# Retention followed by a Fourier-mixing layer on one Trainium2 core: the first batch of the kernel is rebuilt

## The chip, the cores and the metric

The kernel runs on one core of one Trainium2 chip. The metric is the device time of one execution in microseconds (us). The time is the median of several runs; beside it there is one execution taken by the hardware profiler, from which the profile and the trace come.

The engines are named as in the profile: PE is TensorE (matrix products and transposes by an identity), DVE is VectorE, ACT is ScalarE, POOL is GpSimd and SP is SyncE, which here only issues transfers. PSUM is the memory that PE writes to; the other engines read it from there.

## The reference

There are two parts. The first is a recurrent attention over q, k, v of 4 batches x 8 heads x 768 steps x 64 features. The second is a mixing layer on its output x, 768 x 512 per batch. Cut to what is computed:

```python
# for each batch and head; gamma[h] = 1 - 2**(-5-h)
for t in range(768):
    state = gamma * state + outer(k[t], v[t])         # 64 x 64
    y[t] = (q[t] @ state) / 8
x = heads of y side by side                            # 768 x 512
u = x + real(fft(fft(x, axis=seq), axis=feature))
un = (u - mean(u)) / sqrt(var(u) + 1e-6)               # over the 512 features
out = u + relu(un @ w_ch1) @ w_ch2                     # 512 -> 2048 -> 512
```

All inputs and the output are f32. The kernel computes its matrix products in f16 with f32 sums.

## The kernel before

**Attention.** The sequence is cut into 6 chunks of 128 steps, and the 8 heads are taken as 4 pairs in the order 0, 1, 3, 2. For one pair of the first batch: q and k and v are loaded (L171, 384 KB each, on SP's queue), cast to f16 (q at L403, k in two halves with its decay at L412 or L419, v at L428 and L432), q and k are transposed on PE (L444) and copied from PSUM (L452, L455 on ACT). The products k q of each chunk (L469) are masked by the decay on DVE (L476, tile atm). The products k v of the chunks (L491) run through a scan on DVE (L500), which gives the state before each chunk (s16). The output of a head is the sum of atm x v (L515) and q x state (L531) in one PSUM tile, and ACT brings it to the x tile (L544). In the x tile the features 0 to 256 lie forward (side 0) and the others backward (side 1), so that a real transform can be folded.

**The transform.** DVE adds and subtracts the halves of the sequence (fold_s, L684) and the two sides (fold_d, L694). Stage 1 (s1, L741) multiplies the folded x by the tables of cosines and sines over the sequence (csp, ssp), in four groups: cosine and sine, each for two halves of 128 features, and each group in six matmuls 193 wide. The result goes to the f16 tile g (L748 on ACT, L750 on DVE), and reversed to gr (L757). A small product of the edge column (g0_b, L784) gives the features' zero term. Stage 2 (s2, L854 and L858) multiplies a block of 128 rows of g by the tables over the features (cd16, sd16); blocks 0 to 2 of the six row blocks use g and 3 to 5 use gr. In the first batch x is added by PE for blocks 0 to 2 (px, L808, by half identities), and by POOL for the others (L875, L877). ACT copies the odd part (qn, L862, L866), DVE makes u (L867, L869).

**The layer.** The rows of u are centred (mean from an ACT sum, L722 and L728; un, L891), transposed (L945), copied to unT (L947, L948, L950, L952), multiplied by w1 (h0, L978 in the first half of the first batch, L961 later), passed through relu (L985 on ACT, L987 on DVE; L965, L967 later) to ht, and multiplied by w2 (ch, L1000). DVE scales by the deviation and adds u (L1004). In the first half of the first batch the h0 units take one row block at a time: three blocks with four groups of 16 matmuls each, 128 wide. w1 and w2 come in four parts each by transfers that POOL issues (L1154, L1161).

**Tables.** Before, DVE computes the reduced angles in fifteen operations (trig_dve, L294, L296, L298), three for each of five table parts, and ACT takes the absolute value and the sine and cosine (t_act, L322, L326, L331). csp and ssp are stored with even and odd columns apart, so that s1 reads 193 adjacent elements. A second cosine table in natural order, csn (L307), serves g0_b.

**The order.** Everything of the first batch up to its first layer products is listed in first_units(). After each unit pin() ties every instruction to the one before it on its engine, so each engine runs this list in the order that is written. Behind it emit(streams) sorts the units of all batches by due times that are written in the code; the h0 units stand there in the stream "majors" of batch 0. Between units the list holds fillers (L157): matmuls of a zeroed tile (wz, set by POOL at L208) into an unused PSUM tile, forty of them, 512 wide. Batches 1 and 2 take the same transform, batch 3 another form of the layer products; both keep their code, except for what csp and ssp look like. The loads of the first batch are issued in the order q, k, v of each pair. Those of batch 1 (load_unit with `after`) wait for a weight transfer and for an h0 matmul.

These are the lines that set the two table reads:

```python
nc.tensor.matmul(ps[:, par, :], eo[...], tab[:, par, sb, :], ...)   # L741, s1, 193 wide
nc.tensor.matmul(ps[:, kb, :], csn[:, sb, P * kb:P * kb + P], xg[:, sb, :], ...)   # L784
```

Of the kernel before, what the change touches and what calls it, by code (L numbers as in the profile page):

```python
# [18 lines left out]
P = 128  # L19
# [19 lines left out]
NPE = 2  # L39
MIX3 = ((0.005, 0.085, 0.110, 0.125, 0.150), (0.190, 0.290, 0.310, 0.325, 0.350),  # L40
# [9 lines left out]
def kernel(  # L50
# [13 lines left out]
    def pool(name, bufs, **kw):  # L64
# [25 lines left out]
    csp = const.tile([P, 2, 3, NK], f16, tag="csp")  # L90
    ssp = const.tile([P, 2, 3, NK], f16, tag="ssp")
    csn = const.tile([P, 3, 384], f16, tag="csn")
# [9 lines left out]
        "p (n w) -> p n w", n=4)  # L102
    pmask = const.tile([P, 4], f32, tag="pmask")
# [47 lines left out]
    wz = ht16[:, 0:2, :].rearrange("p a b -> p (a b)")[:, 0:DM]  # L151
    wps = ps_w.tile([P, DM], f32, tag="w", name="wps")

    def filler(n):
        def run():
            for _ in range(n):
                nc.tensor.matmul(wps, wz[:, 0:P], wz, start=True, stop=True)  # L157
        return run
# [5 lines left out]
    def load_unit(b, i, after=None):  # L164
        def run():
            h0 = 2 * PAIR_ORDER[i]
            for name, src in srcs.items():
# [18 lines left out]
    for i in range(4):  # L186
        load_unit(0, i)()
# [10 lines left out]
    kf_i = tmp[:, 0, 0:KN].bitcast(i32)  # L198
    kf = tmp[:, 1, 0:KN]
    rs = [tmp[:, 2 + n] if n < 4 else tmp2[:, n - 4] for n in range(10)]  # L200
    icoln = const.tile([P, 5], f32, tag="icoln")
    hpi = const.tile([P, 1], f32, tag="hpi")

    nc.gpsimd.iota(icol_i[:, 0:3], pattern=[[P, 3]], base=0, channel_multiplier=1)
    nc.gpsimd.iota(icol_i[:, 3:5], pattern=[[P, 2]], base=1, channel_multiplier=1)
    nc.gpsimd.iota(icol_i[:, 5:6], pattern=[[0, 1]], base=127, channel_multiplier=-1)
    nc.gpsimd.iota(kf_i, pattern=[[1, KN]], base=0, channel_multiplier=0)
# [5 lines left out]
    nc.vector.tensor_copy(icol[:, 0:6], icol_i[:, 0:6])  # L213
    nc.vector.tensor_scalar(out=gexp[:, 0], in0=lgrow, scalar1=icol[:, 3:4],
                            scalar2=float(math.log(0.125)), op0=ALU.mult, op1=ALU.add)
    nc.vector.tensor_scalar(out=gexp[:, 1], in0=lgrow, scalar1=icol[:, 5:6], scalar2=None,
                            op0=ALU.mult)
    nc.scalar.activation(gexp, gexp, AF.Exp, bias=0.0, scale=1.0)
    for h2 in range(2):
# [3 lines left out]
    make_identity(nc, ident16)  # L223
    nc.gpsimd.affine_select(out=maskf, in_=maskf, compare_op=ALU.is_ge, fill=0.0, base=0,
                            pattern=[[1, P]], channel_multiplier=-1)
    nc.gpsimd.memset(hpi, float(np.pi / 2))
    nc.gpsimd.memset(epsT, 1e-6)
    nc.gpsimd.memset(gk5[:, :, :, 0:1], 0.0)
    nc.vector.tensor_scalar(out=icoln[:, 0:3], in0=icol[:, 0:3],
                            scalar1=float(np.float32(1.0 / S)), scalar2=None, op0=ALU.mult)  # L230
    nc.vector.tensor_scalar(out=icoln[:, 3:5], in0=icol[:, 3:5], scalar1=float(1.0 / DM),
                            scalar2=None, op0=ALU.mult)
    nc.vector.tensor_copy(kf, kf_i)

    def gk_unit(hp):
        def run():
            nc.scalar.copy(gk5[:, hp, :, 1:], gk2[:, hp:hp + 1].unsqueeze(1).to_broadcast(
                [P, D, NCH - 2]))
        return run
# [49 lines left out]
    def trig_dve(idx, n, w, col, coln):  # L289
        r = rs[2 * idx][:, 0:w]  # L290
        ra = rs[2 * idx + 1][:, 0:w]

        def run():
            nc.vector.tensor_scalar(out=ra, in0=kf[:, 0:w], scalar1=coln, scalar2=MAGIC,  # L294
                                    op0=ALU.mult, op1=ALU.add)
            nc.vector.tensor_scalar(out=ra, in0=ra, scalar1=-MAGIC, scalar2=float(n),  # L296
                                    op0=ALU.add, op1=ALU.mult)
            nc.vector.scalar_tensor_tensor(out=r, in0=kf[:, 0:w], scalar=col, in1=ra,  # L298
                                           op0=ALU.mult, op1=ALU.subtract)
        return run  # L300

    def ts_dve(c):
        return trig_dve(c, S, KN, icol[:, c:c + 1], icoln[:, c:c + 1])

    def csn_unit(c):
        def run():
            nc.scalar.activation(csn[:, c, :], rs[2 * c + 1][:, 0:384], AF.Sin, bias=hpi,  # L307
                                 scale=-float(2.0 * np.pi / S))
        return run

    def td_dve(c):
        return trig_dve(3 + c, DM, 257, icol[:, 3 + c:4 + c], icoln[:, 3 + c:4 + c])

    def t_act(idx, part):
        w = KN if idx < 3 else 257
        r = rs[2 * idx][:, 0:w]
        ra = rs[2 * idx + 1][:, 0:w]
        sc = float(2.0 * np.pi / (S if idx < 3 else DM))

        def run():  # L320
            if part == 0:
                nc.scalar.activation(ra, r, AF.Abs, bias=0.0, scale=1.0)  # L322
            elif idx < 3:
                src = (ra, r)[part - 1].rearrange("p (i t) -> p t i", t=2)
                dst = (csp, ssp)[part - 1]
                nc.scalar.activation(dst[:, :, idx, :], src, AF.Sin,  # L326
                                     bias=hpi if part == 1 else 0.0,
                                     scale=-sc if part == 1 else sc)
# [20 lines left out]
    def x_edges(j):  # L349
        def run():  # L350
            nc.gpsimd.memset(xts[j][:, :, :, 0:2], 0.0)
            nc.gpsimd.memset(xts[j][:, :, :, 256:XW], 0.0)
        return run

    def half_ids():
        nc.gpsimd.tensor_scalar(out=hid, in0=ident16, scalar1=0.5, scalar2=1.0, op0=ALU.mult,
                                op1=ALU.mult)
        nc.gpsimd.tensor_scalar(out=nhid, in0=ident16, scalar1=-0.5, scalar2=1.0, op0=ALU.mult,
                                op1=ALU.mult)
# [4 lines left out]
    at, q16_of, kd_of, v16_of, last_cast = {}, {}, {}, {}, {}  # L364

# [33 lines left out]
    def q0_unit(i):  # L399
        def run():  # L400
            q16 = q16_of[0, i] = qzs[i % 2].rearrange("p h c d -> p (h c d)")[
                :, 0:NCH * P].rearrange("p (c h d) -> p c h d", c=NCH, h=2)
            nc.gpsimd.tensor_scalar(out=q16, in0=in_of.pop(("q", 0, i)).rearrange(  # L403
                "p h c d -> p c h d"), scalar1=1.0, scalar2=1.0, op0=ALU.mult, op1=ALU.mult)
        return run

    def k0_unit(i):
        def run():
            h0 = 2 * PAIR_ORDER[i]
            k32 = in_of.pop(("k", 0, i))  # L410
            kd = kd_of[0, i] = kp.tile([P, NCH, 2, D], f16, tag="kd16", name="kd16")
            nc.gpsimd.tensor_scalar(out=kd[:, :, 0, :], in0=k32[:, 0], scalar1=gkd[:, h0:h0 + 1],  # L412
                                    scalar2=1.0, op0=ALU.mult, op1=ALU.mult)
            if i < 3:
                nc.gpsimd.tensor_scalar(out=kd[:, :, 1, :], in0=k32[:, 1],
                                        scalar1=gkd[:, h0 + 1:h0 + 2], scalar2=1.0,
                                        op0=ALU.mult, op1=ALU.mult)
            else:
                nc.scalar.activation(kd[:, :, 1, :], k32[:, 1], AF.Copy, bias=0.0,  # L419
                                     scale=gkd[:, h0 + 1:h0 + 2])  # L420
        return run

    def v0_unit(i):
# [941 lines left out]
```

## Time and profile before

| What | us |
| --- | --- |
| Time, median of 3 runs | 243.88 (243.7 to 243.89) |
| The profiled execution | 244.0 |
| Its span, first to last instruction | 241.8 |
| PE busy | 230.9 |
| DVE busy | 193.0 |
| ACT busy | 126.5 |
| POOL busy | 87.1 |
| First h0 matmul (L978) | 34.77 |
| First ch matmul (L1000) | 48.13 |

All times in the trace count from the start of the span. The profile has several views. The page gives busy shares, the span in 40 slices, and the costliest groups of instructions by line. The table of windows gives, for chosen stretches, each engine's busy time and its number of instructions. The chain of waits follows the work that ended last back from the end, and names at each step what released it. The timeline lists the instructions of an engine in order, neighbours of one kind put together with their number. Matmuls overlap in PE's pipeline, so that the duration of one is longer than the distance from one to the next: at full clock 128 columns start 0.056 us apart, while one lasts 0.22.

### The profile page before, as it was taken

Reading aid. Unit: us, or ns where it says so; the run is one execution under the profiler, and the core shown is the slowest. Engines: PE = TensorE matmul, PEld = TensorE weight load, DVE = VectorE, ACT = ScalarE, POOL = GpSimd, SP = SyncE. Lnnn points to the kernel's source line nnn. Section 1 sums busy time; section 2 is a strip of 40 time slices with the busy share of each in tenths; the row PEclk is TensorE's granted clock in tenths of the full one; section 3 lists DMA queues with packets and bytes.
Section 4 is the critical chain, followed back from the end, with each engine's and each line's share of the span. In section 5 each row is a group of like instructions: output and inputs, shape, how many; then the busy total and the mean of one; then the engine's idle time right before and its main releaser. Section 6 shows DMA issues by size and latency. Waiting matters only on the chain.

```text
span 241.8 us, 5656 instructions
## 1 busy us (share of the span) xinstructions
PE 230.9 (95%) x2160; PEld 155.8 (64%) x2160; DVE 193.0 (80%) x478; ACT 126.5 (52%) x280; POOL 87.1 (36%) x150
## 2 busy tenths in 40 slices
PE   6797899999999999999999999999999999999995
PEld 2354568956676655665567546565567458998884
DVE  8998957898897888996787677899985856768264
ACT  8798669588775435662237522742247305253340
POOL 6667600465600058691000553690000602240302
PEclk9999999999999999999999999999999999999999
DMA  7999999799999567999999758787110141131202
GB/s 172 252 265 146 201 200 202 173 246 236 291 222 228 97 146 167 169 201 126 261 274 222 138 118 234 128 111 173 43 46 0 26 130 43 24 110 24 87 0 89
DMA packets 99466, 36.41 MB, mean 151 GB/s; under 512 B 89840, under 2 KB 96624, under 8 KB 99440
## 3 DMA queue, kind: packets, MB, share of 16 engines
q1 hardware_dynamic: 95072, 31.79, 63.4%
q0 software_dynamic: 4224, 4.19, 10.8%
q8 instruction: 17, 0.28, 0.5%
q10 hardware_dynamic: 144, 0.07, 0.1%
q14 instruction: 9, 0.07, 0.1%
HBM read 27.26 MB, written 6.29 MB: 139 GB/s over the span
## 4 chain that ended last, share of the span: by engine, by line
PE 76%; DVE 6%; SPq 4%; POOL 4%; DMA 3%; ACT 3%; issue 2%; POOLq 0%; ACTq 0%
PE psc L1000 22%; PE psh L961 19%; PE psh L1042 9%; PE psc L1113 7%; SPq L171 4%; PE ps L741 4%; PE wkA L605 3%; DMA q<-in_q_dram 3%; PE psh L978 3%; PE wkY L659 2%; PE wkY L655 2%; PE pq L838 1%; PE wkK L624 1%; PE tq L561 1%; POOL u L877 1%
## 5 line engine op out<-in xcount | busy, mean ns | idle before, releaser
L1000 PE MATMUL psc<-w,ht 128*128 128x512 f16 x288 | 68.3, 379 | 0.0
L961 PE MATMUL psh<-unT,w 128*128 128x384 f16 x320 | 59.5, 326 | 0.0
L875 POOL TENSOR_TENSOR u<-u,x 128x256 f32<-128x256 f32 x21 | 13.5, 643 | 104.9 <-DVE u L845 95.7
L1000 PEld LDWEIGHTS <-ht 128*128 128x128 f16 x288 | 27.1, 98 | 25.7 <-issue 0.2
L961 PEld LDWEIGHTS <-w 128*128 128x128 f16 x320 | 29.9, 98 | 16.0 <-issue 0.6
L965 ACT ACTIVATE ht<-psh 128x384 f16<-128x384 f32 x46 | 22.3, 489 | 24.2 <-PE psh L961 24.0
L608 DVE TENSOR_TENSOR atm<-wkA,maskp 128x512 f16<-128x512 f32 x36 | 23.8, 683 | 1.0 <-PE wkA L605 1.0
L1042 PE MATMUL psh<-unT,w 128*128 128x256 f16 x192 | 21.5, 272 | 0.0
L967 DVE TENSOR_SCALAR ht<-psh 128x384 f16<-128x384 f32 x34 | 18.7, 549 | 2.1 <-PE psh L961 2.1
L895 DVE BATCH_NORM_STATS2 bst<-u 128x6 f32<-128x512 f32 x21 | 14.6, 693 | 7.2 <-POOL u L877 7.1
L1042 PEld LDWEIGHTS <-w 128*128 128x128 f16 x192 | 18.7, 98 | 2.2
L1047 ACT ACTIVATE ht<-psh 128x512 f16<-128x512 f32 x21 | 12.5, 597 | 13.1 <-PE psh L1042 8.2
L634 DVE SCALAR_TENSOR_TENSOR s<-s,gk,wkK 128x128 f16<-128x128 f16 x48 | 16.4, 342 | 2.7 <-ACT s L630 1.9
L1004 DVE SCALAR_TENSOR_TENSOR ob<-psc,stats,u 128x512 f32<-128x512 f32 x18 | 13.4, 744 | 4.9 <-PE psc L1000 4.8
L667 ACT ACTIVATE x<-wkY,gexp 128x384 f16<-128x384 f32 x24 | 12.8, 581 | 8.3 <-PE wkY L659 8.3
L900 ACT ACTIVATE un<-u,stats 128x512 f16<-128x512 f32 x15 | 10.8, 721 | 10.6 <-DVE stats L896 7.1
L388 POOL TENSOR_SCALAR kd<-k,gexp 128x384 f16<-128x384 f32 x24 | 13.9, 590 | 3.8 <-DMA k<-in_k_dram 3.8
L157 PE MATMUL wps<-ht 128*128 128x512 f16 x40 | 12.6, 418 | 2.2 <-POOL ht L208 2.2
L877 POOL TENSOR_TENSOR u<-u,x 128x256 f32<-128x256 f32 x21 | 13.3, 635 | 3.3 <-DVE u L848 2.1
L605 PE MATMUL wkA<-qTz,kT 128*128 128x256 f16 x72 | 13.4, 273 | 0.1
L978 PE MATMUL psh<-unT,w 128*128 128x128 f16 x192 | 11.5, 219 | 0.1
L978 PEld LDWEIGHTS <-w 128*128 128x128 f16 x192 | 11.0, 98 | 0.7 <-issue 0.5
(191 smaller groups left out, 415.6 us busy)
## 6 DMA issues: line engine op xcount, KB each, us to landing
q<-in_q_dram SPq DMA_DIRECT2D x16, 384.0 KB, 6.3
k<-in_k_dram SPq DMA_DIRECT2D x16, 384.0 KB, 5.7
v<-in_v_dram SPq DMA_DIRECT2D x16, 384.0 KB, 6.3
out_dram<-ob SPq DMA_DIRECT2D x18, 256.0 KB, 2.7
w<-in_moe_w_ch_dram POOLq DMA_DIRECT2D x8, 512.0 KB, 10.9
out_dram<-o SPq DMA_DIRECT2D x2, 512.0 KB, 2.9
out_dram<-o SPq DMA_DIRECT2D x3, 128.0 KB, 1.8
unT<-un SPq DMA_TRANSPOSE x15, 2.5
```

The lines of the kernel that those rows point to most:

```text
L605: mm = nc.tensor.matmul(wk[:, c2], st["kT"][:, c, :], st["qT"][:, :, c, :], start=True, stop=True)
L608: nc.vector.tensor_tensor(out=st["atm"][:, 2 * part:2 * part + 2], in0=wk, in1=maskp[:, PAIR_ORDER[i]].unsqueeze(1).to_broadcast([P, 2, 2, ...
L634: nc.vector.scalar_tensor_tensor(out=s16[:, c], in0=s16[:, c - 1], scalar=gk2[:, hp:hp + 1], in1=wk[:, c - c0], op0=ALU.mult, op1=ALU.add)
L877: nc.gpsimd.tensor_tensor(out=u[:, kb, 256:512], in0=u[:, kb, 256:512], in1=x[:, kb, 1, 257:1:-1], op=ALU.add)
L895: nc.vector.bn_stats(bst, u[:, kb, :])
L961: nc.tensor.matmul(psh, w116[:, cb, fb * P:(fb + 1) * P], unT[:, cb, rt * 384:(rt + 1) * 384], start=(cb == 0), stop=(cb == 3))
L965: nc.scalar.activation(ht16[:, fb, :], psh, AF.Relu, bias=0.0, scale=-1.0)
L967: nc.vector.tensor_scalar(out=ht16[:, fb, :], in0=psh, scalar1=-1.0, scalar2=0.0, op0=ALU.mult, op1=ALU.max)
L978: mm = nc.tensor.matmul(psh[:, f], w116[:, cb, fb * P:(fb + 1) * P], unT[:, cb, kb * P:(kb + 1) * P], start=(cb == 0), stop=(cb == 3))
L1000: nc.tensor.matmul(psc, ht16[:, fb, rb3 * P:(rb3 + 1) * P], w216[:, fb, :], start=(fb == 0), stop=(fb == NFB - 1))
L1042: nc.tensor.matmul(psh[:, t], w116[:, cb, fb * P:(fb + 1) * P], unT[:, cb, p * 256:(p + 1) * 256], start=(cb == 0), stop=(cb == 3))
L1113: nc.tensor.matmul(ps[:, c0:c1], lh(f), rh(f)[:, c0:c1], start=first and f == 0, stop=last and f == 7, skip_group_check=True)
```

## The change

It rewrites the first batch; the later batches change only in how s1 and g0_b read the tables.

- *Loads*: the order is now q0 k0 v0 q1 k1 v1 q2 k2 q3 k3 v2 v3.
- *Tables*: PE makes the angles as an outer product of two short rows (tab_unit), DVE or ACT rounds the quotient to an integer in f16 (tn), a second matmul by a scaled identity (nid) subtracts it in PSUM, and ACT takes absolute value and sine from PSUM. The fifteen DVE operations and csn are gone.
- *Table layout*: csp and ssp have all 386 columns in natural order. s1 reads every second element; g0_b reads csp.
- *Block 0*: its centred and transposed tile is summed in PSUM: x by a transposing matmul (stx), the second stage with table and g exchanged (stg), the mean by one matmul (stx4). ACT and DVE each bring one half of it to unT (ste). Its u is still made for the output, but h0 of block 0 doesn't wait for it.
- *Stage 1*: for the outer half of the features the two sides are summed by PE in PSUM (s1s) instead of by fold_d; a negated sine table (nssp) serves the subtraction.
- *px* stays for block 1 only; for the other blocks POOL adds x.
- *Who does what*: a list (ENGINES) gives every cast and copy an engine: P is POOL, A is ACT, D is DVE.
- *Order*: two lists of names, FIRST and SECOND, each pinned; SECOND holds the twelve h0 units, which were in the stream before (where units that do nothing keep their places).
- *Fillers*: eight of 512 columns at the start, behind a memset on DVE, and two later (f512).

```diff
+LOADS = "q0 k0 v0 q1 k1 v1 q2 k2 q3 k3 v2 v3"
+ENGINES = """
+q0:P q1:P q2:P q3:P k00:P k01:P k10:P k11:P k20:A k21:P k30:P k31:A v00:P v10:P v20:A v30:P v31:A
+eq0:D eq1:D eq2:A eq3:A ek00:D ek10:A ek20:A ek30:D ek31:D x00:A x01:A x10:A x11:A x20:A x21:A
+x30:A x31:A tn0:D tn1:D tn2:A tn3:D tn4:D gk0:P gk1:A gk2:A gk3:A gc00a:A gc01a:A gc01b:D gc10a:A
+gc11a:A gc11b:D ste0:D ste1:A xn0:P xn1:D cdh0:P cdh1:D nsp:P hid5:P fs0a:D fs0b:D fla:D flb:D
+fha:D fhb:D fd0:D fd1:D gr0:P gr1:P gr2:D gr3:D nid0:D nid1:D hid:D
+"""
+FIRST = """
+par qz0 hid hid5 gk3 q0 nid0 ta0 gk1 ta1 gk0 tq0 nid1 gk2 tn0 k00 eq0 tb0 si0 k01 v00 tk0 tn1 ab0
...
+sc1 tq2 k20 k21 q3 ae111 eq2 tk2 ae110 tq3 ek20 k30 ae101 am20 am21 ae200 w10 ae201 k31 ae211 yi10
+yi11 ae210 yx1 tk3 w11 x10 ek30 eq3 ek31 ta4 w12 tn4 x11 am30 v30 tb4 am31 v20 ae300 stx01 fs0a
+w13 si4 f512 kv2 fs0b ab4 yi20 ae301 yi21 co4 cdh0 sc2 v31 s1s10 w20 ae310 yx2 kv3 ae311 x20 s1s00
+w21 sc3 x21 yi30 w22 fla yi31 yx3 flb cdh1 x31 w23 fd0 x30 xn1 f512 s1m0 fhb xn0 xm1 stx3 px1 fha
+gc00a g0a fd1 s1s11 qe1 xm0 gr0 s1s01 xm2 s1m1 gc11b gc01a xmb gc11a stg00 xe gc01b gc10a stx4 gr3
+stg01 g0b gr2 s21 g0c stg10 mu1 qn1 mu2 s22 ul1 stg11 qn2 uu1 stx2 ul2 ste1 gr1 un1 ste0 uu2 xl2
+s23 qz1 s20 xu2 qn3 s25 ul3 qn0
+"""
+SECOND = """
+h00 un2 ul0 xl3 uu0 xl0 ut1 uu3 h01 xu0 qn5 uu5 s24 xu3 ul5 h10 qn4 un3 xu5 h11 ul4 xl5 uu4 xl4
+h12 xu4 ut2 h03 un4 h13 h22 h21 h23 h20 h02
+"""
...
-    csp = const.tile([P, 2, 3, NK], f16, tag="csp")
+    csp = const.tile([P, 3, KN], f16, tag="csp")
...
-    nc.gpsimd.memset(wz, 0.0)
-    filler(6)()
+    nc.vector.memset(wz, 0.0)
...
+    for _ in range(8):
+        filler(512)()
...
+            if step == 0:
+                nc.tensor.matmul(ps, tcol[:, idx], trow[:, 0:w], start=True, stop=False, ...)
+            elif step == 2:
+                nc.tensor.matmul(tabs[idx], nid[:, idx // 3], ns[idx][:, 0:w], start=False,
+                                 stop=True, ...)
+            else:
+                scaled(on[f"tn{idx}"], ns[idx][:, 0:w], tabs[idx], float(1.0 / n))
...
     def s1_unit(b, e, cb):
-                                     tab[:, par, sb, :], ...
+                                     tab[:, sb, par:KN:2], ...
...
+    def s1s_unit(e, side):
+            for par in range(2):
+                for sb in range(3):
+                    nc.tensor.matmul(ps[:, par, :], ab[:, par, sb, side, 130:258],
+                                     tab[:, sb, par:KN:2], start=side + par + sb == 0, ...)
...
+    def stg_unit(n, cb):
+            for m in range(4):
+                nc.tensor.matmul(lb[0]["pt"][:, m], wide(n, cb, m),
+                                 fd[0]["g"][:, 2 * n + cb, 0:P], start=False, ...)
...
+    def ste_unit(half):
+            dst, src = (t[:, 2 * half:2 * half + 2] for t in (lb0()["unT"][:, :, 0:P],
+                                                             lb[0]["pt"]))
+            scaled(on[f"ste{half}"], dst, src, -1.0)
```

In the lists q, k, v with a pair (and part) are casts, t transposes, e their copies from PSUM, am and ae the k q products and their masks, kv and sc the k v products and the scan, yi and yx the two halves of the output, x its copy; ta, tn, tb, ab, co, si the steps of a table; fs, fl, fh, fd the folds; s1m and s1s stage 1; gc and gr its copies; xm, xmb and mu the mean; s2, qn, ul, uu, xl, xu, un the steps of one block's u; ut its transposes; w the weights' transfers; and h with block and group the h0 units.

More of the change, by code (lines that the diff above doesn't have):

```diff
@@ L460, in run @@
             st = at[0, i]
-            if half == 0:
-                st["atm"] = ap_.tile([P, NCH, 2, P], f16, tag="atm", name="atm")
             st["wk", half] = wk = [ps_g.tile([P, 3, P], f32, tag="g", name="wkA",
@@ L475, in run @@
             st = at[0, i]
+            if "atm" not in st:
+                st["atm"] = ap_.tile([P, NCH, 2, P], f16, tag="atm", name="atm")
             nc.vector.scalar_tensor_tensor(
@@ L522, in run @@
             st = at[0, i]
-            first = i == 3
-            if first:
-                for h2 in range(2):
-                    st["y", h2] = ps_y.tile([P, NCH, D], f32, tag="y", name="wkY",
-                                            padded_shape=[P, 8, D])
             for c in range(1, NCH):
@@ L1272 @@
     pin()
-    for u in first_units():
-        u()
+    first_of = first_units()
+    for name in FIRST.split():
+        first_of[name]()
+        pin()
+    first.close()
+    ps_pm = pool("ps_pm", 3, space=PSUM)
+    for name in SECOND.split():
+        first_of[name]()
         pin()
     base.update(tails)
-    first.close()
-    ps_pm = pool("ps_pm", 3, space=PSUM)
     late_consts()
```

473 lines of the change are left out of this document (292 added, 181 removed).

## The prediction

> **What bounds the kernel now.** I read the page first: the span and the busy shares (its section 1) and the forty slices (section 2).
>
> ```profile
> PE 230.9 (95%) x2160; PEld 155.8 (64%) x2160; DVE 193.0 (80%) x478; ACT 126.5 (52%) x280; POOL 87.1 (36%) x150
> PE   6797899999999999999999999999999999999995
> DMA  7999999799999567999999758787110141131202
> ```
>
> A slice is 6.05 us. PE is full from the sixth slice to the last but one, so after some 30 us a microsecond off PE's work, or an earlier start of it, is a microsecond off the time. Before that PE waits, and some 10 us of its busy time there is L157's forty fillers (six at 0.457, the others at 0.216). Next I read the table of windows (columns: window, length, then busy time and count of PE, PEld, DVE, ACT, POOL, the clock, the DMA share, GB/s).
>
> ```profile
> 20.00:24.00 4.00, 3.06 (x45) 1.96 (x47) 3.75 (x8) 3.27 (x8) 3.73 (x6) 1.00 0.77 108
> 28.00:34.80 6.80, 6.39 (x55) 4.55 (x56) 5.65 (x17) 3.95 (x12) 0.28 (x1) 1.00 1.24 204
> 34.80:48.10 13.30, 13.05 (x212) 12.22 (x212) 9.71 (x24) 9.96 (x28) 3.31 (x9) 1.00 1.02 186
> 48.10:241.80 193.70, 189.96 (x1627) 127.38 (x1624) 152.07 (x375) 89.18 (x196) 62.87 (x99) 1.00 0.67 138
> ```
>
> The last row is 193.7 us with 190.0 of PE work. The change barely touches it, so what counts is when it begins: the first matmul of L1000, at 48.13 in the timeline. The chain of waits (start, length, what) tells what sets that start.
>
> ```profile
> 11.71 7.67 DMA q<-in_q_dram
> ...
> 19.55 0.83 POOL q16z L403
> 20.38 0.90 POOL w L1154
> 21.33 0.98 POOL kd L412
> 22.31 0.13 issue
> 22.44 0.49 PE tq L444 x6
> ...
> 25.18 0.81 DVE s L500
> 25.99 0.91 DVE atm L476 x2
> ...
> 33.16 0.81 ACT un L891 x2
> 33.98 0.05 issue
> 34.02 0.30 PE pst L945 x2
> ```
>
> So there are three links. A: q3, the tenth load, lands at 19.38; its cast, a weight issue and k3's cast stand in one queue on POOL, then DVE; the last x0 (L544, two of them from 26.90, 1.05 in all) ends at 27.95. B: from there by folds, s1, s2, u, un, transposes and copies to the first h0 matmul (L978) at 34.77, 6.82 us. C: the h0 stretch, 13.36 us. My sum is a new time for each link.
>
> **Link A.** k3 becomes the tenth load and lands when the tenth does, about 19.3. Its halves are cast side by side on POOL and ACT (L412 0.69, L419 0.62), q3 is long cast, and no weight issue (0.8 each) stands before it: 20.0. Six transposes 0.49: 20.5. From there DVE's order is the path. Two half copies of kT3 from PSUM: DVE has no such row; L950 (512 wide, f16, PSUM) took 0.415 and ACT's L452 (768) 0.79, so 0.31 to 0.40 each; I take 0.36, 0.72 for both. The rounding of table 4 (PSUM, 257 wide) lies between L294 (0.34) and L750 (0.60): 0.4. Four mask products start 0.465 apart: 1.86. Two folds of 774 by L684 (0.54 and 0.94): 1.48. Two scans at a step of 0.73: 1.46. Sum 5.9, so 26.4; the ten matmuls of yx3 0.53 and less than two x0, the first of which overlaps, 0.85: **27.8** against 27.95. With all low prices it is 27.4, with the high ones 28.1. v3 now lands last, about 22.5; its halves (0.6) and kv3 (0.47) end by 23.8, before the scan of pair 3 is due.
>
> What the change takes off DVE is fifteen table operations (L294, L296, L298, 0.36 to 1.1 each, 8.6 us), and it adds four roundings (the fifth is ACT's), the copies of q0, q1 and kT0, and kT3's halves: by 0.6 each and 0.72, about 5 us. Before 20 us DVE is over 90% busy, so the cover is thin, but loads land 1.1 to 2.5 apart and that work is not the last to arrive. The ten table matmuls (386 or 257 wide; 512 took 0.216) cost PE 1.5 in time that was filler. Filler falls from forty to ten; no one waits for it. Three csn sines (0.61 each) leave ACT, which takes the casts of k20, v20, v30 and k31 instead.
>
> **Link B.** After the last x0 only the two halves of the last fold (L684, 384 wide, 0.354, step 0.27) are on the path: 0.62. The other folds and the first s1 group come before it, since they need pairs that are done. Then PE has three s1 groups of six (0.085 apart; L741 after 48 us: 72 in 6.81 busy): 1.53; four groups of four 128-wide products into the new PSUM tile, 0.22 each: 0.9; the mean's product, 512 wide: 0.22; g0's nine: 0.23; five blocks of s2 at four matmuls of 0.11: 2.2; one group of x: 0.06. ACT has between the last x0 and the last copy of g three junk sums at a step of 0.72, five copies (a full one 0.60 by L748, quarter-width ones about 0.2), 3.7 in all, up to 31.5. PE is there at 31.0, and at the second group 0.4 early: 0.5 of stalls. Sum 6.25: first h0 at **34.05**, against 34.77. What goes is the row qn, u, un, transposes, copies (31.9 to 34.7); what replaces it, two half evictions (0.4 to 0.6 by L950 and L985), lies beside the last three s2 blocks (1.3), and without them would cost 0.6. POOL's adds to u (0.635) are late for h0 of block 1, not of block 0; block 1's tile is wanted 2.7 us after 34.05.
>
> **Link C.** Before: 192 matmuls at 0.056 are 10.75; s2 of three blocks 1.31; eight transposes 0.45; the rest of 13.36, 0.85, is waiting, most of it at 38.7 to 40.8, where the copy of unT and the relus stood behind qTz memsets (L270, L271, 0.38 each). After: 10.75, one block of s2 0.44, transposes 0.45; the memsets come behind the last relu; I leave 0.2 for waits: 11.84. First L1000 at **45.9**, against 48.13: 2.2 earlier, 0.7 from A and B and 1.5 from C. The two blocks of s2 that move are paid in B, which is counted.
>
> **Behind it.** Batch 1's loads are issued at 44.58 now, held by a weight transfer and an h0 matmul; both come earlier by about 2, and DMA has a hole there. w1's parts land at 25.8, 29.5, 32.0 and 34.6, 2.56 apart. POOL issues them 0.3 to 1 us later relative to the loads that end at 22.5, which fill the engines until then, so landings shift little; h0 of the fourth part starts in the new order after some 5 us of h0. I give back 0.2 because the 3.7 us of PE gaps after 48 us are set partly by transfers and DVE that need not move by the whole amount. Sum: 241.8 - 2.2 + 0.2 = 239.8 of span; the profiled execution was 244.0 with 241.8, 2.2 outside. That gives **242.0**. The median, 243.88, is 0.12 below the profiled execution, within what runs differ.
>
> **The stride.** The tables become contiguous, so s1 reads them with a step of two elements (4 bytes): 72 matmuls in batches 1 to 3 and, in the first batch, 18 on the path. No row has that step. Nearest from below is L741 itself, contiguous: no cost. From above, L531, whose moving operand steps by ten bytes:
>
> ```profile
> 22.87 0.53 PE L531 MATMUL wkY<-s,qTz 64*128 64x64 f16 x10
> 23.87 0.51 PE L469 MATMUL wkA<-qTz,kT 64*128 64x128 f16 x12
> 24.31 0.47 PE L491 MATMUL wkK<-v,kd 128*64 128x64 f16 x10
> ```
>
> Ten strided matmuls took 0.06 more than ten contiguous ones of the same width; taken off the pipeline's end (0.17 to 0.19), pairs are 0.070 to 0.075 apart against 0.056, up to 1.34 times. On 0.085 that is 0.029: 72 are 2.1 and 18 are 0.5. I take nothing, since four bytes is nearer to two than to ten, and keep 2.6 as the upper end.
>
> The Trainium skill, "SBUF — State Buffer", in the note on SBUF cachelines in "Door 1: The DMA port swizzle", says that a line is 16 bytes and that full bandwidth needs at least two accesses to a line, so that up to eight bf16 may be stepped over for free. By its first half a step of 4 bytes has four hits and is free, and ten bytes is not; by the sentence on eight bf16 L531 would have been free, with which its 0.53 against 0.47 does not agree. By either the sum stays 242.0.
>
> **Rivals.**
> 1. *The stride costs* (the slower side). Place: s1 in every batch, PE-bound. At L531's ratio 242.0 + 2.6 = 244.6; it outweighs the gain from 2.0/90 = 22 ns per matmul of 85. For it: s1 is on the PE that bounds. Against it: the step is small. Chance 0.14.
> 2. *The clock falls back.* Thirty of forty fillers go, in the stretch where PE is only 60 to 85% busy with them. The clock rose after 2.74 us of the first fillers (0.457 each, later 0.216). If it is low until the folds, link A's PE pieces double (k3's transposes 0.34, the mask products of pair 3 0.34, yx3 0.3 and kv3 0.3 without their pipeline's end): about 1.3, so 243.3. If it is low through B as well, its 5 us of PE double, of which ACT's stalls hide some: 4.4 in all, 246.4. Against it: with the rows' durations in the new order, PE's longest rest is some 1.9 us, before 10 us, while it waits for loads. Chance 0.12, a fourth of it the second case.
> The Trainium skill, "TensorE: Matmul & The Clock Gate", "HAM oscillation — how this bites in real kernels", says that rests of over about 3.4 us throttle PE; by that rule the clock holds here. The trace of before, with 0.056 between 128-wide matmuls in every stretch after 5 us and no rest that long, agrees, but tests no longer rest.
> 3. *Links A and B give nothing*: DVE's PSUM copies and folds are at their high ends, or the tenth load is 0.5 later, as q3's path was; h00 near 34.8. C alone stays: 244.0 - 1.5 + 0.2 = 242.7, and with new waits in C (relus of 0.6 to 0.68 on two engines, twelve of them among u and un of five blocks) 243.4. Chance 0.14.
> 4. *More than I count*: junk sums hidden, tables early; stalls of 0.5 and the 0.2 given back vanish, and A is at 27.4: 240.9. Chance 0.08.
>
> **The numbers.** Forecast, 241.3 to 242.5, chance 0.52. Faster by over 0.2% is below 243.4, slower is above 244.4, about what a measurement of this kernel can tell from no change. Faster: 0.52 + 0.08 + 0.12 of rival 3 + 0.06 of rival 2 + 0.02 of a cheap stride = 0.80, less 0.06 for mishaps I cannot name: 0.74. Slower: 0.09 of rival 1, 0.03 of rival 2 and 0.03 unnamed, 0.15; the rest, 0.11, is the same. The range goes from 240.9 to 244.4: it leaves out half of rival 4 and the slower cases, under 0.2.
>
> **What would show it.** In the profile after: k3's cast starts near 19.3, not 21.3; last x0 ends at 27.4 to 28.1; first h0 at 33.6 to 34.4; first L1000 at 45.5 to 46.2; s1 of the later batches 0.085 apart; 128-wide matmuls 0.056 apart from 5 us on; the stretch behind L1000 193.7 to 194.1 us. I am wrong if s1's groups take over 0.6 each, if 128-wide matmuls are 0.11 apart after 5 us (the clock row reads 1.00 even over the first fillers, so the spacing tells), if h0 waits for w1, or if the stretch from L1000 on grows by more than half a microsecond.

## The result and the profile after

The changed kernel takes 242.66 us (median of 20 runs, 241.75 to 244.62), the kernel before 243.82 (20 runs): a ratio of 0.9955, with a 95% interval of 0.9938 to 0.9973. A second comparison (e1 below) gave 0.9926, 0.9906 to 0.9946. By the medians it is faster by 1.2 and by 1.9 us, and 1.9 was forecast. The profiled execution took 242.21, with a span of 240.1. Two executions below, one of e5 (1313 us, the profiled one) and one of e6 (472 us), were slow throughout and are left out of what follows.

These are the lines of the page that answer to those of before, with the clock row added, and below them the clock row of before.

```profile
PE 231.2 (96%) x2161; PEld 159.3 (66%) x2161; DVE 189.3 (79%) x484; ACT 122.2 (51%) x273; POOL 89.9 (37%) x149
PE   6888899999999999999999999999999999999995
PEclk9659999999999999999999999999999999999999
```

```profile
PEclk9999999999999999999999999999999999999999
```

PE's work is the same and PE is full a little earlier. What is new is the clock row: in the second and third slice PE is at half clock most of the time (from 7.46 to 17.70 us), which the row of before doesn't show. Ahead of the first rise that is recorded the row reads full whatever the clock was (e11's row has a 9 throughout, and its 128-wide matmuls are 0.106 apart at 11 us), so the spacing of the matmuls has to tell there. Next, the table of windows of the changed kernel:

```profile
9.00:14.00 5.00, 4.79 (x55) 3.43 (x53) 3.67 (x6) 4.36 (x10) 3.19 (x5) 0.50 1.27 251
34.00:46.00 12.00, 12.00 (x207) 11.68 (x205) 10.34 (x23) 6.99 (x15) 5.98 (x10) 1.00 1.19 221
46.00:240.10 194.10, 190.01 (x1618) 127.21 (x1615) 150.94 (x372) 89.72 (x204) 61.76 (x98) 1.00 0.65 136
```

From 9 to 14 us PE seems busier than before (4.79 against 4.50 us), with fewer instructions (55 against 75) and a clock of 0.50. From 34 to 46 it doesn't wait at all. By the links of the prediction (ends of the last x0, first h0 matmul, first matmul of ch, end of the span, all from the timelines):

| | forecast | before | changed | e1 | e4 | e8 |
| --- | --- | --- | --- | --- | --- | --- |
| A: the last x0 ends at | 27.8 | 27.95 | 27.54 | 28.65 | 29.06 | 27.58 |
| B: from there to the first h0 | 6.25 | 6.82 | 6.07 | 6.04 | 6.04 | 6.05 |
| C: first h0 to first ch | 11.84 | 13.36 | 11.83 | 11.82 | 11.82 | 11.60 |
| from the first ch to the end | 193.9 | 193.7 | 194.7 | 194.7 | 194.7 | 194.5 |

C came as forecast and B 0.2 below; B repeats within 0.03, and so does C, but for e8, whose order is another. Link A differs from run to run, and 0.8 more than forecast is given back behind the first ch. The experiments go after these two.

### The profile page after: what moved, and what is told of

It is laid out like the page before. It is cut to its first block, busy times and chain, and to the rows that moved or that the text cites. A ratio compares the mean times of both kernels' runs of the same rounds, so it can differ in the third digit from the quotient of the medians.

```text
span 240.1 us, 5658 instructions
## 1 busy us (share of the span) xinstructions
PE 231.2 (96%) x2161; PEld 159.3 (66%) x2161; DVE 189.3 (79%) x484; ACT 122.2 (51%) x273; POOL 89.9 (37%) x149
## 4 chain that ended last, share of the span: by engine, by line
PE 80%; DVE 6%; ACT 5%; POOL 3%; DMA 2%; issue 2%; SPq 0%; ACTq 0%; POOLq 0%
PE psc L1157 22%; PE psh L1118 19%; PE psh L1199 9%; PE psc L1270 8%; PE psh L1135 4%; PE wkA L622 3%; PE ps L760 3%; PE wkY L676 2%; DMA k<-in_k_dram 2%; PE wkY L672 1%; PE pq L952 1%; ACT qTz L584 1%; PE wkK L641 1%; PE pq L1006 1%; PE tq L468 1%
## 5 line engine op out<-in xcount | busy, mean ns | idle before, releaser
L989 POOL TENSOR_TENSOR u<-u,x 128x256 f32<-128x256 f32 x18 | 11.6, 645 | 99.2 <-DVE u L959 98.0
L1118 PEld LDWEIGHTS <-w 128*128 128x128 f16 x320 | 29.9, 98 | 16.0 <-issue 0.6
L1199 PE MATMUL psh<-unT,w 128*128 128x256 f16 x192 | 21.5, 272 | 0.0
L1199 PEld LDWEIGHTS <-w 128*128 128x128 f16 x192 | 18.7, 98 | 2.2
L1161 DVE SCALAR_TENSOR_TENSOR ob<-psc,stats,u 128x512 f32<-128x512 f32 x18 | 13.4, 745 | 6.9 <-PE psc L1157 6.7
L991 POOL TENSOR_TENSOR u<-u,x 128x256 f32<-128x256 f32 x18 | 11.4, 635 | 2.7 <-DVE stats L1056 1.8
L954 ACT COPY qn<-pq 128x128 f32<-128x128 f32 x18 | 4.9, 274 | 12.4 <-PE pq L952 12.3
L622 PEld LDWEIGHTS <-kT 128*128 128x128 f16 x72 | 6.8, 98 | 6.3 <-ACT kT L589 0.4
```

The costliest lines, as they stand in the source:

```text
L622: mm = nc.tensor.matmul(wk[:, c2], st["kT"][:, c, :], st["qT"][:, :, c, :], start=True, stop=True)
L1118: nc.tensor.matmul(psh, w116[:, cb, fb * P:(fb + 1) * P], unT[:, cb, rt * 384:(rt + 1) * 384], start=(cb == 0), stop=(cb == 3))
L1199: nc.tensor.matmul(psh[:, t], w116[:, cb, fb * P:(fb + 1) * P], unT[:, cb, p * 256:(p + 1) * 256], start=(cb == 0), stop=(cb == 3))
```

## The experiments

### e1: what varies from run to run

The changed kernel, unchanged.

> The changed kernel once more, unchanged, to see which stretch carries the spread of its times (241.75 to 244.62, while the kernel before keeps within 243.5 to 244.8). Theory one: two things vary independently, the number of 3.4 us windows at half clock before 20 us, and the landing of k3, the tenth load. Then a run of about 243.2 at clock 1.00 has k3's cast near 19.3 and the first L1157 matmul near 46.6, and a run of about 242.2 at clock 0.978 has them near 18.1 and 45.4, as in the first profile. Theory two: the stretch behind the first L1157 matmul varies (194.7 in the first profile, 193.7 before); then the first L1157 matmul stays at 45.4 and the rest takes up to 196.

Measured: 242.22 (6 runs, 241.88 to 243.43). The profiled execution is one of the late ones, 243.32. Its first ch comes at 46.51 instead of 45.44, and the stretch behind it is 194.7 as in the first profile. So what varies between these two executions lies before the first ch: theory two falls. But theory one holds only in part, since k3's cast starts at 18.12, early. What is late is that the clock falls a second time, from 21.4 to 24.8 us, between k3's landing and the fold; link A ends 1.1 later.

### e4: five more fillers

```diff
-... ta1 gk0 tq0 nid1 gk2 tn0 k00 eq0 tb0 si0 ... tn1 ab0 ek00 tb1 co0
+... ta1 gk0 tq0 f512 f512 nid1 gk2 tn0 k00 eq0 tb0 f512 f512 si0 ... tn1 ab0 ek00 tb1 f512 co0
```

> The changed kernel with five more fillers of 512 columns between 5 and 8 us, where PE is busy a third of the time. They lie in PE's waits for q0's and k0's copies. Both theories expect the clock at 1.00 in most runs. If the half clock costs the time, the median goes down to 241.9. If the clock costs little, because the loads cover it, and the runs at 243.2 with clock 1.00 have a later k3, the median goes up to 243.2.

Measured: 243.76 (10 runs, 243.35 to 244.89), ratio to before 0.9991 (0.9978 to 1.0005). More fillers early keep the clock up there and take nearly the whole gain away. Two things differ in the profiled execution. The first shows in the timelines of POOL: first the changed kernel, then e4, at the cast of k3's first half (start, length, and in brackets how long POOL idled and what ended that):

```profile
18.06 0.58 POOL L194 TENSOR_SCALAR kd<-k,gexp 128x384 f16<-128x384 f32 x1 [0.87 <-DMA k<-in_k_dram]
```

```profile
19.43 0.58 POOL L194 TENSOR_SCALAR kd<-k,gexp 128x384 f16<-128x384 f32 x1 [2.23 <-DMA k<-in_k_dram]
```

k3 lands 1.4 later. The transfers in the traces show what goes with it. A load comes in sixteen pieces, one for each DMA engine. In e4 fifteen of k3's pieces land by 17.91 and the last at 19.34. Nearby, a queue for instructions (q8, which I take for PE's) moves 16 KB, and this takes 1.1 to 1.3 us:

| | fetch at | tenth load lands | eleventh | twelfth |
| --- | --- | --- | --- | --- |
| e4 | 15.50 | 19.34 | 20.96 | 22.29 |
| before | 16.05 | 19.38 | 21.14 | 22.46 |
| e3 | 16.06 | 19.41 | 21.10 | 22.41 |
| e1 | 17.00 | 18.04 | 21.05 | 22.38 |
| e10 | 17.00 | 18.47 | 21.02 | 22.34 |
| changed | 17.06 | 17.97 | 21.13 | 22.47 |
| e7 | 18.85 | 18.08 | 19.86 | 22.44 |
| e8 | 18.92 | 18.18 | 19.96 | 22.50 |
| e12 | 20.58 | 18.19 | 20.00 | 21.63 |

(e3 and the runs from e7 on are described below.) The later the fetch, the later the first load that is held up: the tenth, the eleventh, the twelfth, and in e12 none of them; the loads behind it are late as well. When the fetch comes is less clear. A full clock, with which PE gets through its program sooner, would bring it forward; but e9 and e10 give PE the same matmuls up to there, with a full clock from 13.3 and 13.6 on, and fetch at 18.92 and 17.00.

The second thing is the clock. In e4 it fell from 21.94 to 25.35, behind a stretch in which PE waits for k3. Every run of e4 has a mean clock of 0.993 or less, and one spell of 3.41 us at half clock makes 0.993, so none went without one. How much each of the two costs is told by k3's transposes on PE, in the changed kernel and in e4:

```profile
19.45 0.51 PE L468 MATMUL tq<-ident,kd 128*128 128x128 f16 x6
```

```profile
20.18 0.49 PE L468 MATMUL tq<-ident,kd 128*128 128x128 f16 x6 [1.06 <-ACT kd L193]
```

They are only 0.7 later, since in the changed kernel they stand in PE's order behind pair 2's output, and DVE copies them at 20.79 instead of 20.34. So of the 1.5 by which link A is longer (29.06), the late k3 makes 0.45 directly and the rest, 1.1, comes while the clock is down.

### e7 and e6: no early fillers, and late ones

e7 leaves the first eight fillers out; e6 adds four at 19.5 to 21.

```diff
-    for _ in range(8):
-        filler(512)()
```

> The changed kernel without its eight early fillers. Theory: PE's instruction fetch (16 KB, 1.3 us) takes one DMA engine from a load. At 15.5 to 16.1 us it delays the tenth load, k3, by 1.4 (e3, e4, kernel before); at 17.0 only the eleventh (first profile, e1). Sixteen instructions fewer make PE ask about 1 us later, so that k3 lands at 18.0 in each run, whatever the clock: no run at 243.2, median 242.0 to 242.4. If the landing has nothing to do with the fetch, k3 lands at 18.0 or 19.4 as before. If the clock is what counts, PE is cold from the start and the median goes up by 0.5 to 1.

Measured: 243.24 (6 runs, 242.08 to 243.62). The fetch moved to 18.85, and now the eleventh load isn't late either, but the twelfth, as the table shows: the landing goes with the fetch. The median is not what was expected. In the profiled execution (243.62) the clock fell from 21.5 to 24.9, and link A ended late again, at 28.86; three of the six runs have the mean clock of 0.993 that goes with one such spell. PE was at half clock until 18.0 in this execution, and k3's cast was as early as ever.

```diff
-yi11 ae210 yx1 tk3 w11 x10 ek30 eq3 ek31 ta4 w12
+yi11 ae210 yx1 f512 f512 tk3 w11 x10 ek30 eq3 ek31 ta4 f512 f512 w12
```

> The changed kernel with four more fillers, two ahead of k3's transposes and two ahead of pair 3's mask products (19.5 to 21), where PE waits. They stand behind the instructions whose fetch hits a load, so k3's landing doesn't change by them. If the half clock between 21 and 25 us (e1) is what makes the slow runs, the runs above 243.5 go; those at 243.2, with full clock early and a late k3, stay. No gain for runs that already had a full clock there.

Measured: 242.68 (5 runs, 242.36 to 243.49). No run is above 243.5, but e1 had none there either, so the times say little alone. The mean clock says more: these runs have 1.00 or 0.978, which is the early spell of 10.24 us alone, and the 27 runs of e8 to e11, with the same late fillers, have 0.998 or more, where three of six had 0.993 in e7 without them.

### e5 and e8: block 5 ahead, and the three edits together

e5 takes un of block 5 out of the later stream and puts it behind the last h0 unit.

```diff
-h12 xu4 ut2 h03 un4 h13 h22 h21 h23 h20 h02
+h12 xu4 ut2 h03 un4 h13 h22 h21 h23 h20 h02 un5
...
-                s2s, unTs = [], [unTs[0], norm_unit(0, 5)] + unTs[1:]
+                s2s = []
```

> The changed kernel with un of block 5 ahead of the root of the deviation on ACT, behind the last h0 unit. In all four profiles of the changed kernel and its variants the stretch behind the first L1157 matmul is 194.7 long, against 193.7 before. Theory: 0.8 of it come from block 5, whose un stands behind an ACT table load and the roots (48.1 to 50.3); its transposes and with them batch 1's come after 30 L1157 matmuls instead of 20, and PE then waits on ACT from 53 to 58. With this edit the transposes come after 20 again, and the stretch shrinks to 193.9 to 194.0; median 0.7 to 0.8 under the changed kernel's 242.2 to 242.7. Rival: the 1.0 is the stride or transfers; then the stretch stays at 194.7.

Measured: 242.25 (5 runs, 241.66 to 243.57). There is no profile of these, so e8 has to answer for the stretch.

> The edits of e5, e6 and e7 together: no early fillers, four late ones, un of block 5 ahead. By the theories k3 lands at 18.0, the clock is full from 21 us on, and the stretch behind the first L1157 is 0.7 to 0.8 shorter: 241.2 to 241.6, with the runs close together. By the rivals, no better than e7.

Measured: 242.33 (6 runs: three at 241.8 to 241.9 and three at 242.8 to 243.0), ratio to before 0.9915 (0.9895 to 0.9934). In the profiled execution, 241.87, k3's cast is early, the clock is full from 14.1 on without a fall, and the first ch comes at 45.23. The first h0 comes at 33.63 instead of 34.89 in e7. Of these 1.26, DVE's copies of k3's transposes already make 0.37 (20.34 against 20.71), ahead of the late fall; the other 0.9 comes with it. The stretch behind the first ch is 194.5, not 194.0. Its order is as wanted. PE's timeline in the changed kernel, then in e8:

```profile
45.44 2.75 PE L1157 MATMUL psc<-w,ht 128*128 128x512 f16 x12
48.03 0.39 PE L1105 MATMUL pst<-ident,un 128*128 128x128 f16 x4
48.25 4.05 PE L1157 MATMUL psc<-w,ht 128*128 128x512 f16 x18
52.14 0.39 PE L1105 MATMUL pst<-ident,un 128*128 128x128 f16 x4
52.36 0.50 PE L578 MATMUL tq<-ident,q16z 128*128 128x128 f16 x6
```

```profile
47.40 1.89 PE L1155 MATMUL psc<-w,ht 128*128 128x512 f16 x8
49.13 0.39 PE L1103 MATMUL pst<-ident,un 128*128 128x128 f16 x4
49.35 1.03 PE L1155 MATMUL psc<-w,ht 128*128 128x512 f16 x4
50.22 0.50 PE L576 MATMUL tq<-ident,q16z 128*128 128x128 f16 x6
```

In the changed kernel batch 1's transposes (tq) wait for 30 ch matmuls, in e8, as before, for 20 (eight stand ahead of the lines shown). So more ch matmuls are left to fill PE's waits for batch 1's copies. Only 0.2 to 0.3 came of it, a third of what I put it at.

### e9: the support work of batch 1

```diff
-h12 xu4 ut2 h03 un4 h13 h22 h21 h23 h20 h02 un5
+h12 xu4 ut2 qt0 h03 un4 qt1 h13 mk0 qt2 h22 mk1 qt3 h21 mk2 h23 mk3 h20 h02 un5
```

Here mk makes two of the eight mask copies on ACT, and qt zeroes a quarter of qTz on POOL; both are gone from behind SECOND.

> e8 with the mask copies (eight on ACT, 1.7 us) and the four zeroings of qTz (from DVE to POOL) taken into the h0 stretch, where ACT has 5 us and POOL 6 us free. In the kernel before they ran there; in the changed kernel and e8 they stand behind the last h0 unit and ahead of batch 1's copies. If they are what is given back behind the first L1157 matmul, that stretch goes from 194.5 (e8) to 194.1 to 194.2, what the stride alone leaves (194.2 in e2), and the profile's end moves by 0.3 to 0.4. If the rest of the loss is transfers, it stays at 194.5.

Measured: 242.09 (4 runs, 241.83 to 242.13), ratio to before 0.9906 (0.9893 to 0.9919). The stretch is 194.6, so the expectation missed. Part of this is no loss of PE's: from DVE's last operation to the end of the span it takes 2.80 instead of 2.50 (in e10 too), and up to the last matmul the stretch is 0.16 shorter than in e8. The timeline tells where the rest went: the first h matmul of the second half (L961 in before at 64.36) comes at 61.30, a lead of 3.06, more than the 2.9 at the first ch, where e8 has 62.02. Then PE waits for a load of batch 1:

```profile
63.51 0.51 PE L576 MATMUL tq<-ident,kd 128*128 128x128 f16 x6 [0.42 <-POOL kd L421]
```

The support work did hold PE up: matched with before, PE's lead shrinks by 0.74 between 52 and 58 us in e8, and not at all in e9. Behind it stands the next limit, the loads: the last four of batch 1 landed only 2.1 to 2.3 ahead of before, and the lead is 2.46 at 70 us. Link C stays 11.61 (11.60 in e8) with this work back in the h0 stretch, the zeroings on POOL instead of DVE, so it need not have moved behind. This is the best version tried, and the one whose runs lie closest together, though its lead over e8 is within what e8's runs differ.

### e2 and e10: the stride

e2 is the kernel before with the table layout of the change:

```diff
-    csp = const.tile([P, 2, 3, NK], f16, tag="csp")
+    csp = const.tile([P, 3, KN], f16, tag="csp")
...
-                                     tab[:, par, sb, :], start=(sb == 0), stop=(sb == 2))
+                                     tab[:, sb, par:KN:2], start=(sb == 0), stop=(sb == 2))
```

> The kernel before with one part of the change: cosine and sine tables in natural order, so that s1 steps by two elements in every batch (96 matmuls). By the first profile of the changed kernel, whose later 72 matmuls kept PE busy for 7.07 us against 6.81, a step of two costs 3.6 ns per matmul: 0.3 to 0.4 us in all, about 244.2. By the rival of the prediction it is up to 29 ns: 2.6 us, 246.4. If only the first batch set the difference, 243.8.

Measured: 244.41 against 244.13 (11 and 22 runs): 1.0013, 1.0003 to 1.0023, or 0.1 to 0.6 us. It costs, but little. e10 takes the stride out of e9 for batches 1 to 3: the sine table is stored with even and odd columns apart, and POOL makes such a copy of the cosine table during h0 (in room that the view calls gk).

```diff
-                                     tab[:, sb, par:KN:2], start=(sb == 0), stop=(sb == 2))
+                                     tab[:, par, sb, :], start=(sb == 0), stop=(sb == 2))
```

> e9 with the tables of stage 1 contiguous for batches 1 to 3 (sine table stored with even and odd columns apart from the start, a copy of the cosine table made by POOL during h0). By e2 the stride costs 0.3 to 0.5 us: the stretch behind the first L1157 matmul goes to 193.7, PE busy there for 6.81 instead of 7.07 in s1. If e2's difference was noise, nothing moves.

The groups by form of PE behind 48 us, in e9 and then in e10 (busy us, mean ns):

```profile
L758 PE MATMUL ps<-ssp,ee 128*128 128x193 f16 x36 | 4.2, 251 | 0.0
L758 PE MATMUL ps<-csp,ee 128*128 128x193 f16 x36 | 4.2, 251 | 0.0
```

```profile
L762 PE MATMUL ps<-gk,ee 128*128 128x193 f16 x36 | 4.1, 248 | 0.0
L762 PE MATMUL ps<-ssp,ee 128*128 128x193 f16 x36 | 4.0, 247 | 0.0
```

That is 3 to 4 ns per matmul. Matched matmul by matmul with before, the changed kernel, e2, e8 and e9 each lose 0.08 to 0.09 in the s1 groups of every later batch, 0.25 in all, and e10 loses nothing there: its lead is 1.72 at 64 us and 1.72 at 237. The time, 242.32 (5 runs, 241.63 to 242.56), doesn't show it, since in the profiled execution k3 lands 0.3 later and the first ch comes at 45.81, 0.56 later than in e9.

### e11: the cover of the evictions

```diff
-s23 qz1 s20 xu2 qn3 s25 ul3 qn0
...
-h00 un2 ul0
+h00 s23 qz1 s20 xu2 qn3 s25 ul3 qn0 un2 ul0
```

> e8 with the last three s2 blocks behind the first h0 unit instead of ahead of it, so that nothing covers the two evictions of block 0's tile. By the prediction that cover is worth about 0.6: the first h0 matmul comes at about 32.9 instead of 33.6, and the first L1157 matmul at 45.8 instead of 45.2. If the evictions cost PE nothing, 45.2.

Measured: 243.99 (12 runs, 243.03 to 244.39). The first h0 comes 6.04 behind the last x0, as in e8, although three s2 blocks less stand before it:

```profile
33.11 0.22 PE L845 MATMUL pst<-ident,ht 128*128 128x128 f16 x1
34.48 1.05 PE L1132 MATMUL psh<-unT,w 128*128 128x128 f16 x16 [1.15 <-DVE unT L193]
```

From first h0 to first ch it is 12.92 against 11.60. So the cover is worth 1.3, not 0.6. The chain of waits goes through ACT's sums and copies to 31.8, and DVE's reversal and three steps of u, which stand ahead of its eviction (34.09): PE and this chain end together. The other 0.9 comes ahead of link B: the last x0 ended at 28.44, in an execution whose clock was full only from 18.1 on. Pair 2's masks are 0.55 late there already (18.86 against 18.31 in e8), although k3 lands 0.1 earlier.

### e3 and e12: two parts undone

e3 gives back the loads by pairs, e12 (on e8) makes the angles by fifteen DVE operations at the places of the roundings.

```diff
-LOADS = "q0 k0 v0 q1 k1 v1 q2 k2 q3 k3 v2 v3"
+LOADS = "q0 k0 v0 q1 k1 v1 q2 k2 v2 q3 k3 v3"
```

> The changed kernel with the loads by pairs again: v2 goes ahead of q3 and k3. If k3's landing sets link A, k3 comes one load (1.7 us) later, and the first h0 matmul and the end move by 1.2 to 1.7 against the changed kernel: about 244.0. If DVE's queue sets link A and the load is hidden, nothing moves: 242.7.

Measured: 246.93 (6 runs, 245.93 to 247.31), first h0 at 37.33. In PE's timeline q3's transposes, which stand ahead of pair 2's mask products, wait for the load that is now the tenth:

```profile
20.47 0.82 PE L468 MATMUL tq<-ident,q16z 128*128 128x128 f16 x6 [3.65 <-POOL q16z L194]
```

So pair 2's masks start at 21.76 instead of 18.47 and DVE copies k3's transposes at 24.00 instead of 20.34, which is the whole delay of 3.7 in this execution. The clock fell in that time as well, from 20.22 to 23.64, at the end of PE's rest. The profiled execution is the fastest; four of the other five have a mean clock of 0.958 and no profile, so what a low clock adds in them is open.

```diff
-                nc.tensor.matmul(ps, tcol[:, idx], trow[:, 0:w], start=True, stop=False, ...)
...
+                nc.vector.tensor_scalar(out=ra, in0=kf[:, 0:w], scalar1=jcoln[:, idx:idx + 1],
+                                        scalar2=MAGIC, op0=ALU.mult, op1=ALU.add)
+                nc.vector.tensor_scalar(out=ra, in0=ra, scalar1=-MAGIC, scalar2=float(n), ...)
+                nc.vector.scalar_tensor_tensor(out=t, in0=kf[:, 0:w], scalar=jcol[:, idx:idx + 1],
+                                               in1=ra, op0=ALU.mult, op1=ALU.subtract)
```

> e8 with the reduced angles made by fifteen DVE operations again (8.6 us) instead of outer products and roundings, at the places of the roundings. The tables are the same up to rounding. By the prediction the loads cover most of it before 20 us, but the fifth table stands on link A's path between kT3's copies and the mask products, with 1.9 to 2.4 us instead of 0.4: the first h0 matmul 1.5 to 2 later than e8's 33.6, about 243.5. If DVE's room ends earlier, more than 2; if the path isn't DVE's, 0.

Measured: 246.96 (4 runs), first h0 at 39.15. The first h0 is 3.7 later than in the changed kernel in e3 and 5.5 later than in e8 in e12, where 1.2 to 1.7 and 1.5 to 2 were expected. Most of it has one reason in both: the pinned order is built around the part that is gone. In e12 the chain of waits shows it.

```profile
12.03 4.07 issue
16.10 0.04 POOLq L194
16.14 0.33 POOL ht L194
16.47 0.80 issue
17.27 0.84 POOL v L194
```

The negation of the sine table (ht here) stands on POOL ahead of v1's cast and waits for a table that DVE now makes later. v1's cast starts at 17.27 instead of 13.67 in the changed kernel, and pair 1 with it. By kT3's copies e12 is 3.8 behind e8 (24.10 against 20.34). The rest, 1.8, comes behind them: the fifth table takes DVE 1.1 instead of 0.3 there, and the clock falls from 27.85 to 31.26.

## Why the prediction was right, and where not

**Right, by its own steps.** Link B: 6.25 forecast, 6.04 to 6.07 in four profiles. Link C: 11.84 forecast, 11.82 to 11.83. What brings the first ch forward is that the row from qn to the copies of unT is gone and that s2 blocks moved ahead; e11 tests the second, while no run gives back the first, which is read from the chain of waits. The memsets had to leave DVE at most, not the stretch: e9 brings them back on POOL, and the mask copies with them, and C stays 11.61. The profiled execution has the span of the forecast within 0.3 (240.1 against 239.8): the sum of A 0.3 better, B 0.2 better and the part behind 0.8 worse. Two of the four signs by which the prediction would be wrong did appear: 128-wide matmuls 0.11 apart after 5 us, and a stretch behind the first ch that grew by more than half a microsecond. The first cost little in this execution, and A and B made up for part of the second.

**The step that was mis-sized: "I give back 0.2."** It is 1.0 in every profile of the changed kernel and of the variants with its order. Of this, 0.25 is the stride, which I took at nothing (e2, e10; of the bounds, 0 and 2.6, the lower was near). 0.2 to 0.3 is block 5's place behind the roots (e8 against e7). The rest I counted as a gain of link C without a price: the memsets and mask copies "come behind the last relu", where they stand ahead of batch 1's copies. e9 takes them away and PE's lead then holds to 61 us, until it runs into batch 1's loads. How large these three are next to each other in the changed kernel itself stays open, since taking one away lets the next appear.

**Link A was half luck.** I had k3's landing set the path: 19.3, and with it DVE at k3's transposes (kT3's copies) at 20.5. It didn't set it. This is the chain of waits of the changed kernel there:

```profile
18.48 1.54 DVE atm L501 x4
20.02 0.31 issue
20.34 0.19 DVE kT L194
```

k3 lands at 17.97, and DVE comes to its transposes at 20.34, because until then it masks pair 2. The second half of the sum, 7.3 from there to the last x0, is right at full clock:

| | kT3's copies start | from there to the last x0 | half clock |
| --- | --- | --- | --- |
| forecast | 20.5 | 7.3 | never after 5 us |
| changed | 20.34 | 7.21 | 7.5 to 17.7 |
| e8 | 20.34 | 7.25 | until 14.1 |
| e6 | 20.59 | 7.24 | 8.0 to 18.3 |
| e10 | 20.63 | 7.55 | until 13.6 |
| e11 | 20.89 | 7.56 | until 18.1 |
| e1 | 20.39 | 8.27 | 7.8 to 18.0, 21.4 to 24.8 |
| e7 | 20.71 | 8.14 | until 18.0, 21.5 to 24.9 |
| e4 | 20.79 | 8.28 | 21.9 to 25.4 |

Only in e4 of these does the chain go through k3's landing. What makes the runs that took 243.2 with a clock of 1.00 on record stays open. A late k3 alone gives 0.45. A half clock from the start is another candidate, since the record begins with the first rise: e11 is recorded with 1.00 too, and in e3, with the same first fillers as the changed kernel, the clock rose only at 13.4. None of these runs was profiled.

**The rival of the clock.** The clock did fall, to which I gave 0.12. My reason against it, that PE's longest rest would be 1.9, was no reason: in the changed kernel no rest from 4.05 to 7.46 is over 0.67, and the clock fell at 7.46. Its price, 1.3, was near for a fall that lies on link A's end: from 21 to 25 us it costs 0.6 to 1.1 by the table. Before 18 us it costs between nothing (the changed kernel) and 0.5 (e7 and e11 against e8) by kT3's copies, where loads set part of the pace. The Trainium skill, "TensorE: Matmul & The Clock Gate", says in "Part 1: The HAM clock gate" that the clock is set by free-running windows of 3413 ns. With this the traces agree: the spells at half clock are 10.24 and 3.41 us long, three windows and one. Its rule in "HAM oscillation — how this bites in real kernels", rests of over 3.4 us, fits the fall in e3, in a rest of 3.65, but not the others: the clock falls without such a rest too.

**The rival of the stride** pays 0.25, not 2.1, in the later batches, far from the 22 ns per matmul from which it would decide: it is 3 to 4. The row with ten bytes was a poor neighbour for one of four. The Trainium skill, "SBUF — State Buffer" (note on cachelines in "Door 1: The DMA port swizzle"), by which this step is free, is nearly right: 4% of a matmul of 85 ns.

**The evictions' cover** was put at 0.6, by their own length. It is 1.3 (e11), because what stands ahead of them on DVE and ACT counts too.

## What to carry to other kernels

When work is taken off a stretch by moving it behind, find what it then stands ahead of, and price that: here up to 0.75 of 2.7 us came back that way. In a stretch that waits for loads, look which wait ends last before you put a load's landing into the sum: k3 landed 1.4 earlier than I thought, and DVE came to it at nearly the time that I had. More work for PE there isn't always a gain either: e4 lost the clock later, where it counts more. And an order pinned around one transfer order or table maker can't be judged by undoing that part alone, since the rest of the order then waits for it.

## What the hardware showed that was not expected

- With a fetch of 16 KB of instructions one load's last piece comes some 1 to 1.4 us behind the others, and the loads behind it are late as well: the tenth for fetches at 15.5 to 16.1 us, the eleventh at 17.0 to 17.1 (21.13 against 19.86 in e7), the twelfth at 18.9 (22.44 against 21.63 in e12).
- The clock can fall without a long rest. It fell behind windows in which PE's columns, at full clock, fill about 0.33 (e4, 21.9 us), 0.4 (changed, 7.5 us) or 0.6 (e1, 21.4 us) of the time, and it held behind others at 0.47 to 0.6, so the bound isn't settled. (The share is the columns of the matmuls that start in a window, at 0.42 ns each, over 3.41 us.) Windows at 0.65 and over were not followed by a fall in any profile here.
- A moving operand that steps by four bytes costs 3 to 4 ns on 85.
